# The queries of batch 2 turned by DMA instead of on TensorE, in issues between those of its keys

## The chip, the cores and the metric

The kernel runs on one core of a Trainium2 chip. Times are microseconds of the device for one execution. The engines are TensorE (PE in the profile, with its weight loads as PEld), VectorE (DVE), ScalarE (ACT), GpSimd (POOL) and SyncE (SP). GpSimd and SyncE also issue the transfers: GpSimd those that cast while they load, SyncE the stores and the transfers that transpose.

## The reference

```python
def _attn_ref(q, k, v):                      # q, k, v: (8, 8, 576, 64)
    scores = scale * np.matmul(q, k.transpose(0, 1, 3, 2))
    mask = (rel >= 0) & (rel < 64)           # rel = query position - key position
    scores = np.where(mask, scores, -1000000000.0)
    scores = scores - np.max(scores, axis=-1, keepdims=True)
    attn = np.exp(scores)
    attn = attn / (np.sum(attn, axis=-1, keepdims=True) + 1e-09)
    return np.matmul(attn, v)

def _moe_ref(x, w_in, w_out):                # (4608, 512), (512, 2048), (2048, 512)
    h = x @ w_in
    g = h * np.cos(h)
    return g @ w_out
```

A causal attention with a window of 64 over 8 batches of 8 heads and 576 positions, then two products over all 4608 rows with `h * cos(h)` between them. The input of the second part is the attention's output with the heads side by side. Inputs and output are float32.

## The kernel before

The 4608 rows are worked in nine tiles of 512 (`mt`, `MT`). For each, the first product (`first`, line 500) makes 16 blocks of 128 columns of h, ScalarE makes the sine (730), VectorE multiplies (733, the gate), and the second product (744) makes the output rows, which VectorE or ScalarE copy out and SyncE stores (509). TensorE does this without a pause while the attention of a later batch is worked between the products.

The attention of a batch goes so. GpSimd loads q, k and v in chunks of 128 positions (`load_chunk`, 183; `load_v`, 189), chunk 4 having 64. q and k are turned, so that a head's 64 numbers lie on the partitions. The scores come in two bursts (`burst_scores`, 331), the first for the query blocks 0 to 3 of 64 positions, the second for 4 to 8; a query block meets its own key block and the one before. VectorE adds the mask and takes the maximum (368), ScalarE the exponential and its sum (380), VectorE the reciprocal (390), GpSimd normalizes (397), SyncE transposes the weights by DMA (416), and TensorE multiplies them with v (`values`, 432).

q and k are turned in two ways. `turn` (244) is a DMA transpose that SyncE issues; three make one tensor of a batch, for the chunks 0 and 1, 2 and 3, and 4 (`TURNS`). k of batches 2 to 7 (`turn_k`) and q of batches 3 to 7 (`turn_q`, those in `TURNED`) go that way. q of batch 2 is transposed on TensorE: for each of four pairs of heads `tr_q` makes five transposes (227) into PSUM, and `put_q` copies them into place with two copies of VectorE (127). The turned q of a batch lies in one of two tiles, `qsets[b % 2]`; batch 2 takes that of batch 0 (`qT_75` in the order of instructions; that of the odd batches is `qT_76`).

The order of the opening (batches 0 and 1, and the first tile) is written out by hand in `FIRST`. After it, steps are entered with a due time (`at`), in which a tile has `T` = 32 units, 16 for each of its products, and `pump` writes those that are due into the program as the products go by. Each engine then takes its instructions in that order. The steps that were due before the main loop starts, the three turns of k of batch 2 among them, are written at its start, at tile 1.

SyncE and GpSimd hold their transfers in program order: one that waits for its data holds up those behind it. A transfer also waits for the landing of the one eight issues before it on the same engine.

Of the kernel before, what the change touches and what calls it, by code (L numbers as in the profile page):

```python
# [30 lines left out]
PAIRS = 4  # L31
Q = 16
T = 2 * Q
# [5 lines left out]
BUSY = 8  # L39
NB = 5  # L40
TURNS = ((0, 2), (2, 4), (4, 5))
TURNED = (3, 4, 5, 6, 7)
FAST = (7, 8)
PRODUCTS = ("P1", "P2", "P6", "P5", "P7", "P3", "P4")

# [26 lines left out]
def kernel(  # L72
# [9 lines left out]
    nc = tc.nc  # L82
    B, H, S, D = q.shape
# [17 lines left out]
    qsets = [const.tile([128, NB * PAIRS * 128], BF16, name=f"qT{i}") for i in range(2)]  # L101
# [5 lines left out]
    ident = const.tile([128, 128], BF16, name="ident")  # L107
# [6 lines left out]
    st = {}  # L114
# [11 lines left out]
    def copy(engine, out, in_):  # L126
        {"a": nc.scalar.copy, "p": nc.gpsimd.tensor_copy}.get(engine, nc.vector.tensor_copy)(out, in_)  # L127
# [29 lines left out]
    def head_rows(name, b, p):  # L157
        if (name, b) not in st:
            st[name, b] = rows_tile(name)
        lo = 2 * NC * D * p if b else RC * D + 2 * NC * D * (p - 1)  # L160
        return st[name, b][0:NP, lo:lo + 2 * NC * D].rearrange("p (h x) -> p h x", h=2)
# [48 lines left out]
    def transposed(name, b, p):  # L210
        t_ps = ps_t.tile([128, S], BF16, tag="t", name=f"t{name}_ps")
        of = st[name, b]
        if b == p == 0:
            for c in range(RC):
                for h in range(2):
                    d = slice(64 * h, 64 * h + 64)
                    nc.tensor.transpose(t_ps[d, 64 * c:64 * c + 64], of[d, 64 * c:64 * c + 64], ident[d, d])
        elif b < 2:
            rows = head_rows(name, b, p)
            for c in range(NC):  # L220
                for h in range(2):
                    nc.tensor.transpose(t_ps[64 * h:64 * h + 64, NP * c:NP * c + NP], rows[:, h, D * c:D * c + D],  # L222
                                        ident[:NP, :NP])
        else:
            for c in range(NB):
                n = min(128, S - 128 * c)
                nc.tensor.transpose(t_ps[:, 128 * c:128 * c + n], of[0:n, c, 128 * p:128 * p + 128], ident[0:n, 0:n])  # L227
        return t_ps


    def in_order(t_ps, to, b, p):
        c = RC if b == p == 0 else NC
        return t_ps.rearrange("d (c p) -> d p c", c=c), to.rearrange("d (p c) -> d p c", c=c)

    def by_pair(x):
        return x[:, 0:PAIRS * S].rearrange("d (h s) -> d h s", h=PAIRS)

    def by_chunk(x):
        return x.rearrange("d (c h p) -> d c h p", c=NB, h=PAIRS)
# [12 lines left out]
    def tr_q(b, p):  # L252
        st["tq", b, p] = transposed("q", b, p)

    def put_q(b, p, engine=None):
        if b > 1:
            t_ps, to = st.pop(("tq", b, p)), by_chunk(qsets[b % 2])[:, :, p]
            copy(engine, to[:, 0:4], t_ps[:, 0:512].rearrange("d (c p) -> d c p", c=4))
            copy(engine, to[:, 4, 0:64], t_ps[:, 512:S])
            return  # L260
        of, to = in_order(st.pop(("tq", b, p)), by_pair(qsets[b])[:, p], b, p)
        if b:
            copy(engine, to, of)
        elif engine == "a":
            nc.scalar.mul(to, of, scale)
        else:
            nc.vector.tensor_scalar(to, of, scale, None, ALU.mult)
# [4 lines left out]
    def tr_k(b, p):  # L272
        st["tk", b, p] = transposed("k", b, p)
# [327 lines left out]
    def at(time, fn, *args):  # L601
        plan.append((time, len(plan), fn, args))
# [25 lines left out]

    for b in range(2, B):
        t0 = T * (b - 1)  # L630
        for lo, hi in TURNS if b in TURNED else ():
            at(t0 - T + (24.3 if b == 4 else 23.4) + 0.01 * lo, turn_q, b, lo, hi)
        for p in range(0 if b in TURNED else PAIRS):
            t_q = t0 + (2 if b == 2 else 1) + (3.3 if b == 2 else 3.5) * p
            at(t_q, tr_q, b, p)
            at(t_q + 0.02, put_q, b, p)
        if b > 2:
            for c in range(NB):
                for i, name in enumerate(("q", "k")):
                    time = 17.9 + 2.8 * i if b == 3 and c == NB - 1 else 5.6 + 1.6 * c + 0.8 * i  # L640
                    if b > 3 and name == "k" and c > 2:
                        time = (24.2 if b == 4 else 22.4) + 0.01 * c
                    if b > 4 and c == 0:
                        time = (24.26 if b == 5 else 22.46) + 0.01 * i - T
                    at(t0 - T + time, load_chunk, name, b, c)
        for lo, hi in TURNS:
            at(t0 + 0.1 * lo - (2 if b == 2 else 6), turn_k, b, lo, hi)
        for c in range(5):
            at(t0 + (8 if b == B - 1 else 0.5) + c, load_v, b, c)
        for half_ in range(2):  # L650
            if b == 2:
                at(t0 + 24.1 + 0.01 * half_, spread_v, b, half_, "p", 0, 2)
                at(t0 + 24.2 + 0.1 * half_, spread_v, b, half_, "p", 2, 4)
            else:
                at(t0 + (24 if b == 3 else 22.2) + 0.1 * half_, spread_v, b, half_)
# [27 lines left out]
    def spread_first(lo, hi):  # L683
# [9 lines left out]
             "io": put_steps, "mk": put_masks, "mc": cast_masks,  # L693
             "tq": lambda p: tr_q(0, p), "tk": lambda p: tr_k(0, p), "Tq": lambda p: tr_q(1, p), "Tk": lambda p: tr_k(1, p),
             "pq": lambda p, engine: put_q(0, p, engine), "pk": lambda p, engine: put_k(0, p, engine),
             "Pq": lambda p, engine: put_q(1, p, engine), "Pk": lambda p, engine: put_k(1, p, engine),
             "zA": spread_first(0, 1), "zB": spread_first(1, 3), "zC": lambda engine: spread_v(0, 1, engine, 3, 4),
             "yA": lambda engine: spread_v(1, 0, engine, 0, 2), "yB": lambda engine: spread_v(1, 0, engine, 2, 3),
# [85 lines left out]
```

## Time and profile before

| | us |
|---|---|
| three runs | 301.02, 301.63, 302.92 |
| median | 301.63 |
| the profiled execution | 301.49 |
| its span, first to last instruction | 299.7 |
| mean granted clock of TensorE | 0.998 |

Where tile 1 and tile 2 lie in the span, from the timeline of TensorE:

| stretch | from, us | to, us |
|---|---|---|
| first product of tile 1, with the transposes of q of batch 2 | 57.23 | 72.98 |
| second product of tile 1, with both bursts of scores of batch 2 | 72.98 | 88.77 |
| values for tile 2 | 88.77 | 90.00 |
| first product of tile 2 | 90.00 | 103.90 |
| second product of tile 2, with the bursts of batch 3 | 103.90 | 119.24 |

In the profile's timelines a row has the start, the length, the engine (with a q for its sequencer or the queue of transfers that it issues), the line, the operation, the tiles as out<-in, and a count; what stands in brackets is idle time before it and what ended it. For a transfer the length is that of the issue; how long it takes to land stands in a line of its own. In a view of one line of the kernel the three numbers of a row are the least, the median and the largest duration in ns, and those behind them the first and the last start.

### The profile page before, as it was taken

The numbers are of one execution on the slowest core, as the hardware profiler recorded it, in microseconds if no ns is written. First come the engines' busy times: TensorE is split into PE (matmuls) and PEld (weight loads), VectorE is DVE, ScalarE is ACT, GpSimd is POOL, SyncE is SP. The second block draws the span as 40 slices with busy tenths as digits, with TensorE's granted clock in tenths as the row PEclk, the third lists the DMA queues.
The fourth block names the chain that finished last, engine by engine and source line by source line (L and its number), as shares of the span: only waits on it lengthen the run. The fifth ranks groups of instructions, "written<-read, shape, count | busy, mean of one in ns | idle before, by whom it ended". The sixth has DMA issues, their size and how long they took to land.

```text
span 299.7 us, 8184 instructions
## 1 busy us (share of the span) xinstructions
PE 291.8 (97%) x2787; PEld 159.7 (53%) x2787; DVE 230.9 (77%) x904; ACT 232.3 (77%) x781; POOL 205.2 (68%) x226
## 2 busy tenths in 40 slices
PE   8978999999999999999999999999999999999995
PEld 3667854544454444444454545444544454784584
DVE  4998788988887786788677866887588658976793
ACT  5997699876988799869986998699969996305600
POOL 9898668993699849995999599949997850000000
PEclk9999999999999999999999999999999999999999
DMA  7999999999999995999999999999999443003013
GB/s 147 175 204 191 196 190 141 113 138 148 234 165 121 202 175 99 167 143 229 152 171 139 178 164 199 142 230 165 152 121 189 70 88 142 0 3 140 3 35 107
DMA packets 165867, 43.22 MB, mean 144 GB/s; under 512 B 153216, under 2 KB 161472, under 8 KB 165824
## 3 DMA queue, kind: packets, MB, share of 16 engines
q0 software_dynamic: 100896, 18.06, 81.6%
q1 hardware_dynamic: 64784, 24.56, 45.7%
q8 instruction: 22, 0.36, 0.5%
q14 instruction: 21, 0.17, 0.2%
q10 hardware_dynamic: 144, 0.07, 0.1%
HBM read 36.70 MB, written 9.44 MB: 154 GB/s over the span
## 4 chain that ended last, share of the span: by engine, by line
PE 89%; DMA 6%; POOL 2%; DVE 0%; issue 0%; POOLq 0%
PE h_ps L500 37%; PE out_ps L744 28%; PE out_ps L587 8%; PE out_ps L483 5%; DMA w_in<-in_moe_w_in_dram 4%; PE h_ps L464 4%; PE o_ps L432 3%; PE s_ps L331 3%; DMA q<-in_q_dram 2%; POOL v L189 1%; PE s_ps L353 1%; PE tq_ps L227 0%; POOL w_in L205 0%; PE tw_ps L413 0%; POOL q L166 0%
## 5 line engine op out<-in xcount | busy, mean ns | idle before, releaser
L500 PE MATMUL h_ps<-xT,w_in 128*128 128x512 bf16 x512 | 112.5, 379 | 0.2
L733 DVE TENSOR_TENSOR gT<-h_ps,sin 128x512 bf16<-128x512 f32 x128 | 84.9, 688 | 27.3 <-ACT sin L730 27.3
L730 ACT ACTIVATE sin<-h_ps 128x512 f32<-128x512 f32 x128 | 73.8, 598 | 34.8 <-PE h_ps L500 32.6
L380 ACT ACTIVATE e<-s,negm 128x128 f32<-128x128 f32 (+1 forms) x256 | 97.2, 382 | 1.7 <-POOL v L127 0.9
L397 POOL TENSOR_TENSOR w<-e,rden 128x512 bf16<-128x512 f32 (+1 forms) x68 | 69.0, 1029 | 28.8 <-DVE rden L390 21.1
L744 PE MATMUL out_ps<-w_out,gT 128*128 128x512 bf16 x384 | 85.3, 379 | 0.0
L500 PEld LDWEIGHTS <-w_in 128*128 128x128 bf16 x512 | 49.7, 98 | 58.3
L744 PEld LDWEIGHTS <-gT 128*128 128x128 bf16 x384 | 36.5, 98 | 43.1
L368 DVE CUSTOM_DVE_ANT_0 s<-s_ps,mask 128x128 f32<-128x128 f32 (+1 forms) x256 | 56.0, 276 | 1.8 <-PE s_ps L353 1.5
L380 ACT ACTIVATION_READ_ACCUMULATOR e<-s,negm 128x1 f32 x256 | 48.3, 189 | 0.0
L189 POOL DMA_DIRECT2D v<-in_v_dram x40 | 34.1, 877 | 0.6 <-DMA q<-in_q_dram 0.6
L183 POOL DMA_DIRECT2D q<-in_q_dram x30 | 26.4, 883 | 4.6 <-PE tq_ps L222 2.6
L183 POOL DMA_DIRECT2D k<-in_k_dram x30 | 26.3, 886 | 0.6 <-DMA v<-in_v_dram 0.6
L390 DVE RECIPROCAL rden<-den 128x4 f32<-128x4 f32 (+1 forms) x73 | 12.2, 167 | 18.4 <-ACT e L380 18.1
L127 POOL COPY v<-v 64x1536 bf16<-64x1536 bf16 (+3 forms) x16 | 22.9, 1431 | 0.4
L368 DVE DVE_READ_ACCUMULATOR2_ANT negm<- 128x1 f32 x256 | 21.0, 82 | 0.1
L127 DVE CAST xT<-o_ps 128x512 bf16<-128x512 f32 x24 | 15.5, 677 | 4.7 <-PE o_ps L432 4.5
L464 PE MATMUL h_ps<-xT,w_in 128*128 128x256 bf16 x128 | 14.6, 273 | 0.9 <-DMA w_in<-in_moe_w_in_dram 0.9
L483 PE MATMUL out_ps<-w_out,gT 128*128 128x512 bf16 x64 | 14.8, 380 | 0.0
L464 PEld LDWEIGHTS <-w_in 128*128 128x128 bf16 x128 | 12.3, 98 | 2.3 <-DMA w_in<-in_moe_w_in_dram 1.0
L587 PEld LDWEIGHTS <-sums 128*128 128x128 bf16 x136 | 12.2, 98 | 2.0 <-DVE sums L532 0.4
L470 ACT ACTIVATE sin<-h_ps 128x512 f32<-128x512 f32 x16 | 9.2, 596 | 4.3 <-PE h_ps L464 4.3
(92 smaller groups left out, 293.0 us busy)
## 6 DMA issues: line engine op xcount, KB each, us to landing
out_dram<-out_sb SPq DMA_DIRECT2D x16, 512.0 KB, 8.0
v<-in_v_dram POOLq DMA_DIRECT2D x32, 128.0 KB, 6.2
q<-in_q_dram POOLq DMA_DIRECT2D x24, 128.0 KB, 9.5
k<-in_k_dram POOLq DMA_DIRECT2D x24, 128.0 KB, 9.4
w_in<-in_moe_w_in_dram POOLq DMA_DIRECT2D x4, 512.0 KB, 8.7
w_out<-in_moe_w_out_dram POOLq DMA_DIRECT2D x4, 512.0 KB, 10.9
q<-in_q_dram POOLq DMA_DIRECT2D x7, 144.0 KB, 6.2
k<-in_k_dram POOLq DMA_DIRECT2D x7, 144.0 KB, 6.3
```

Of the source, the lines that this page charges most:

```text
L127: {"a": nc.scalar.copy, "p": nc.gpsimd.tensor_copy}.get(engine, nc.vector.tensor_copy)(out, in_)
L183: nc.gpsimd.dma_start(out=st[name, b][0:n, c].rearrange("p (h d) -> p h d", h=H), in_=src.rearrange("h p d -> p h d"))
L189: nc.gpsimd.dma_start(out=vt.rearrange("p (h d) -> p h d", h=H), in_=v[b, :, c * 128:c * 128 + n, :].rearrange("h p d -> p h d"))
L368: nc.vector.tensor_tensor_reduce(out=s[:, u, c], in0=s_ps[:, u, c], in1=mask[:, 2 - j % 2 if j else 0, c], scale=-scale if b else -1.0, sc ...
L380: nc.scalar.activation(e[:, u, c], s[:, u, c], AF.Exp, bias=negm[:, u:u + 1], scale=1.0 if n < n_first else -1.0, accum_out=den[:, u:u + 1])
L397: (nc.gpsimd if engine == "p" else nc.vector).tensor_tensor(out=w[:, 0:u], in0=e[:, 0:u], op=ALU.mult, in1=rden[:, 0:u].unsqueeze(2).to_br ...
L464: nc.tensor.matmul(out=h_ps[:, half * e:half * e + half], lhsT=w_in_sb[:, ks, ff * 128:ff * 128 + 128], rhs=st["xT", 0][:, ks, half * g:ha ...
L500: nc.tensor.matmul(out=st["h", ff], lhsT=w_in_sb[:, ks, ff * 128:ff * 128 + 128], rhs=st["xT", mt][:, ks], start=start, stop=stop)
L587: nc.tensor.matmul(out=to[n_] if split else to[:, e], lhsT=lhs[name][f // 2][:, f % 2, 128 * e:128 * e + 128], rhs=rhs[name][:, f, lo:hi], ...
L730: nc.scalar.activation(sin, h_ps, AF.Sin, bias=math.pi / 2.0)
L733: nc.vector.tensor_tensor(out=gt[:, e], in0=h_ps, in1=sin, op=ALU.mult)
L744: nc.tensor.matmul(out=o_ps[e], lhsT=gT[ff // 2][:, ff % 2, ms * 128:ms * 128 + 128], rhs=w_out_sb[:, ff], start=ff == 0, stop=ff == n_ff - 1)
```

## The change

q of batch 2 is turned by DMA like those of the later batches. The list of batches to turn goes away, and with it the transposes of chunks in `transposed` and the copies in `put_q` that only batch 2 used. Each of the three turns of q of batch 2 gets a due time 0.01 before that of the turn of k of the same chunks, so that they alternate; the due times of the other batches are as before.

```diff
-TURNED = (3, 4, 5, 6, 7)
...
-        elif b < 2:
+        else:
             rows = head_rows(name, b, p)
...
-        else:
-            for c in range(NB):
-                n = min(128, S - 128 * c)
-                nc.tensor.transpose(t_ps[:, 128 * c:128 * c + n], of[0:n, c, 128 * p:128 * p + 128], ident[0:n, 0:n])
         return t_ps
...
     def put_q(b, p, engine=None):
-        if b > 1:
-            t_ps, to = st.pop(("tq", b, p)), by_chunk(qsets[b % 2])[:, :, p]
-            copy(engine, to[:, 0:4], t_ps[:, 0:512].rearrange("d (c p) -> d c p", c=4))
-            copy(engine, to[:, 4, 0:64], t_ps[:, 512:S])
-            return
...
     for b in range(2, B):
         t0 = T * (b - 1)
-        for lo, hi in TURNS if b in TURNED else ():
-            at(t0 - T + (24.3 if b == 4 else 23.4) + 0.01 * lo, turn_q, b, lo, hi)
-        for p in range(0 if b in TURNED else PAIRS):
-            t_q = t0 + (2 if b == 2 else 1) + (3.3 if b == 2 else 3.5) * p
-            at(t_q, tr_q, b, p)
-            at(t_q + 0.02, put_q, b, p)
+        for lo, hi in TURNS:
+            at(t0 - (2.01 - 0.1 * lo if b == 2 else T - (24.3 if b == 4 else 23.4) - 0.01 * lo), turn_q, b, lo, hi)
```

The queue of SyncE, from the last weights of the opening (`wT`) to the weights of the first burst of batch 2, before:

```order
L416 DMA_TRANSPOSE wT<-w 128x4x128
L244 DMA_TRANSPOSE kT<-k 128x8x128 x2
L244 DMA_TRANSPOSE kT<-k 128x4x64
L416 DMA_TRANSPOSE wT<-w 128x4x128 x2
L509 DMA out_dram<-out_sb 128x2x512 x2
L416 DMA_TRANSPOSE wT<-w 128x4x128 x4
```

and now, in the changed program, whose lines are ten fewer up to here:

```order
L406 DMA_TRANSPOSE wT<-w 128x4x128
L239 DMA_TRANSPOSE qT_75<-q 128x8x128
L239 DMA_TRANSPOSE kT<-k 128x8x128
L239 DMA_TRANSPOSE qT_75<-q 128x8x128
L239 DMA_TRANSPOSE kT<-k 128x8x128
L239 DMA_TRANSPOSE qT_75<-q 128x4x64
L239 DMA_TRANSPOSE kT<-k 128x4x64
L406 DMA_TRANSPOSE wT<-w 128x4x128 x2
L499 DMA out_dram<-out_sb 128x2x512 x2
L406 DMA_TRANSPOSE wT<-w 128x4x128 x4
```

The three turns of q have come in, one ahead of each turn of k; all that follows stands three transfers later.

VectorE in the first product of tile 1, from the last normalizing of batch 1 to the first scores of batch 2, before:

```order
L397 TENSOR_TENSOR w<-e,rden 128x512
L733 TENSOR_TENSOR gT<-h_ps,sin 128x512 x4
L127 COPY qT_75<-tq_ps 128x4x128
L127 COPY qT_75<-tq_ps 128x64
L733 TENSOR_TENSOR gT<-h_ps,sin 128x512 x3
L127 COPY qT_75<-tq_ps 128x4x128
L127 COPY qT_75<-tq_ps 128x64
L733 TENSOR_TENSOR gT<-h_ps,sin 128x512 x3
```

and now:

```order
L126 COPY out_sb<-out_ps 128x512
L387 TENSOR_TENSOR w<-e,rden 128x512
L380 RECIPROCAL rden<-den 128x4
L387 TENSOR_TENSOR w<-e,rden 128x512
L719 TENSOR_TENSOR gT<-h_ps,sin 128x512 x16
L358 ISA s,negm<-s_ps,mask 128x64
```

The eight copies of q have gone, and the sixteen gate products follow one another. On TensorE the four groups of five transposes have gone from between the products of the same stretch.

## The prediction

> **What bounds the kernel now.** I read the page's busy shares and the chain of work that ended last, then the timeline of TensorE around the place of the change.
>
> ```profile
> PE 291.8 (97%) x2787; PEld 159.7 (53%) x2787; DVE 230.9 (77%) x904; ACT 232.3 (77%) x781; POOL 205.2 (68%) x226
> PE 89%; DMA 6%; POOL 2%; DVE 0%; issue 0%; POOLq 0%
> ```
>
> TensorE is busy 291.8 of 299.7 us, and 89% of the chain is its own work. What leaves its queue in the steady part shortens the kernel by the time it took there, if nothing makes TensorE wait instead. The timeline of TensorE (start, length, line, count) shows what leaves:
>
> ```profile
> 57.23 2.75 PE L500 MATMUL h_ps<-xT,w_in 128*128 128x512 bf16 x12
> 59.82 0.52 PE L227 MATMUL tq_ps<-ident,q 128*128 128x128 bf16 x5
> 60.27 3.63 PE L500 MATMUL h_ps<-xT,w_in 128*128 128x512 bf16 x16
> 63.73 0.52 PE L227 MATMUL tq_ps<-ident,q 128*128 128x128 bf16 x5
> 64.18 2.76 PE L500 MATMUL h_ps<-xT,w_in 128*128 128x512 bf16 x12
> ...
> 72.98 0.59 PE L331 MATMUL s_ps<-kT,qT 64*64 64x64 bf16 x32
> 73.51 6.22 PE L744 MATMUL out_ps<-w_out,gT 128*128 128x512 bf16 x28
> 79.65 0.86 PE L331 MATMUL s_ps<-kT,qT 64*64 64x128 bf16 x40
> ...
> 88.77 1.20 PE L432 MATMUL o_ps<-wT,v 128*64 128x64 bf16 x64
> ```
>
> There is no idle time in brackets on any of these rows. The consumers of what is turned are the two bursts of scores of batch 2, at 72.98 and 79.65, and its values at 88.77.
>
> **The change, part by part.** *The transposes leave TensorE.* From the start of a group of five to the start of the next product it is 60.27 - 59.82 = 0.45 and 64.18 - 63.73 = 0.45 us (0.52 reaches to the modelled end of the last, which overlaps). Four such groups, two of them shown, give 1.80 us, all on the path: **-1.8 us**. That is the whole gain on offer, 0.6% of the time.
>
> *What comes next on TensorE, closed up.* Five banks of h rotate in this product, so its sixth column block needs the first gate product. I look at the rows of ScalarE and VectorE there.
>
> ```profile
> 58.79 1.28 ACT L730 ACT_TABLE_LOAD   x1
> 60.09 2.71 ACT L730 ACTIVATE sin<-h_ps 128x512 f32<-128x512 f32 x5
> 63.07 0.60 ACT L730 ACTIVATE sin<-h_ps 128x512 f32<-128x512 f32 x1 [0.27 <-PE h_ps L500]
> 60.72 2.48 DVE L733 TENSOR_TENSOR gT<-h_ps,sin 128x512 bf16<-128x512 f32 x4 [1.00 <-ACT sin L730]
> L127 DVE COPY qT<-tq_ps 128x512 bf16<-128x512 bf16 x4 | 1.6, 411 | 0.0
> ```
>
> The first sine waits for a table load until 60.09, whatever TensorE does. The first gate product ends at about 61.4 (one of the four takes 2.48 / 4 = 0.62 after 60.72). TensorE reaches the sixth block five blocks after 57.23: a block is four products, 3.63 / 16 x 4 = 0.9, less overlap (12 in 59.82 - 57.23 = 2.59, so 0.86 each), hence at 57.23 + 4.32 = 61.55. It fits by 0.1 us; I book 0. From 63.07 ScalarE waits 0.27 us for TensorE before a sine, so it follows a faster TensorE. VectorE loses four copies of 0.41 us and four small ones; it waits for sines here, so this is worth nothing by itself.
>
> *Three turns come onto SP's queue.* Its rows before, in the order of issue (start, length, count):
>
> ```profile
> 43.70 8.34 SPq L416 DMA_TRANSPOSE wT<-w  x6
> 61.36 6.30 SPq L244 DMA_TRANSPOSE kT<-k  x3
> ...
> 70.34 1.21 SPq L509 DMA_DIRECT2D out_dram<-out_sb  x2
> 78.05 5.88 SPq L416 DMA_TRANSPOSE wT<-w  x4
> ```
>
> SP is free from 52.04 to 61.36. q's first turn (chunks 0 and 1) stands ahead of k's first and can go at 52; k's first still waits until 61.3 for k's chunk 1, which is loaded here:
>
> ```profile
> L183 POOL DMA_DIRECT2D k<-in_k_dram x1: 903/903/903, 55.2 to 55.2; - x1
> DMA to landing us min/median/max: 6.1/6.1/6.1
> ```
>
> 55.2 + 6.1 = 61.3. q's first turn thus costs the later ones nothing on SP, but moves its data at about 53 to 57 beside k's loads. How full the DMA engines are there and later (a row's last two numbers are the share of their time that packets took, with overlaps, and GB/s):
>
> ```profile
> 54.00:58.00 4.00, 4.00 (x87) 2.62 (x86) 3.55 (x15) 2.58 (x9) 4.00 (x6) 1.00 1.53 97
> 70.00:74.00 4.00, 4.00 (x52) 1.92 (x50) 3.28 (x7) 2.69 (x5) 1.36 (x2) 1.00 2.53 142
> ```
>
> Bounds for what the turn delays the landing of chunk 1: 0 (it is done first) to 2.4 us (it has the engines to itself for as long as a two-chunk turn takes, below). At 1.53 they are less crowded than the 2.53 of later: I take 0.5, near the lower end.
>
> The other two q turns stand between the k turns. The three k turns, each one's row with its time to landing:
>
> ```profile
> L244 SPq DMA_TRANSPOSE kT<-k x1: 1247/1247/1247, 61.4 to 61.4; - x1
> DMA to landing us min/median/max: 6.8/6.8/6.8
> ...
> L244 SPq DMA_TRANSPOSE kT<-k x1: 2759/2759/2759, 62.7 to 62.7; - x1
> DMA to landing us min/median/max: 10.2/10.2/10.2
> ...
> L244 SPq DMA_TRANSPOSE kT<-k x1: 2099/2099/2099, 65.6 to 65.6; - x1
> DMA to landing us min/median/max: 8.5/8.5/8.5
> ...
> L416 SPq DMA_TRANSPOSE wT<-w x2: 1216/1222/1227, 67.8 to 69.1; - x2
> DMA to landing us min/median/max: 7.3/7.4/7.4
> ```
>
> They land at 68.2, 72.9 and 74.1, the weights behind them at 75.2 and 76.4. So turns overlap, one queue in order: a two-chunk turn takes 4.7 us of it beside the loads, the short one 1.2, and a turn of weights, half a two-chunk one, 1.2, so 2.4 for a two-chunk turn in a quieter stretch. The six turns of batch 3 are a second measure:
>
> ```profile
> L244 SPq DMA_TRANSPOSE qT<-q x3: 1195/1231/1243, 84.1 to 86.9; - x3
> L244 SPq DMA_TRANSPOSE kT<-k x3: 1243/1267/2392, 88.2 to 92.1; - x3
> DMA to landing us min/median/max: 3.3/4.5/5.3
> ```
>
> From the first issue at 84.1 to at most 92.1 + 5.3 = 97.4 it is 13.3 us for six, 2.2 each. Added ahead of the last k turn are one two-chunk turn (2.2 to 4.7 us; I take 3.0, between them and nearer the low end, since POOL's loads, which made the crowd, stop before 72, as its row further down shows) and one short turn (1.1 to 1.2). With the 0.5 above, the last k turn lands at 74.1 + 0.5 + 3.0 + 1.1 = 78.7; bounds 74.1 + 2.2 + 1.1 = 77.4 and 74.1 + 2.4 + 4.7 + 1.2 = 82.4.
>
> *When it is needed.* Both bursts come 1.8 us sooner. The first, at 71.2, needs chunks 0 and 1 of both: k's land at 68.2 + 0.5, so 2.5 us of cover are left. (It started at 72.98 while k's last turn was still to land at 74.1, so it waits only for the chunks that it reads.) The second starts at 79.65 - 1.8 = 77.85, and reads chunk 4 last, in its last 8 of 40 products, so at about 77.85 + 0.7 = 78.5. Against 78.7 that is a stall of 0.2 us; bounds 0 and 3.9. **+0.2 us.**
>
> *What is queued behind.* The two weight turns and the two stores go 2 to 3 us later. The weights are read at 88.77 and landed by 76.4. The first of the stores frees the buffer that takes the third pair of rows of the running tile:
>
> ```profile
> L509 SPq DMA_DIRECT2D out_dram<-out_sb x2: 509/556/602, 70.3 to 71.0; - x2
> DMA to landing us min/median/max: 7.8/8.7/9.5
> ```
>
> They landed at 70.3 + 7.8 = 78.1 and 71.0 + 9.5 = 80.5, and would at about 81 and 83.5. The copy into that buffer follows 48 products, 28 of them before the second burst and 20 after it (6.22 / 28 = 0.22 each), so it comes at 79.65 + 0.86 + 4.4 - 1.8 = 83.1, after the first store. Then come the four weight turns of the first burst, at 78.05 to 82.7:
>
> ```profile
> L416 SPq DMA_TRANSPOSE wT<-w x1: 1189/1189/1189, 82.7 to 82.7; - x1
> DMA to landing us min/median/max: 3.7/3.7/3.7
> ```
>
> The last lands at 86.4 and is read at 88.77: cover 2.3 us. Issue and use both move up by 1.8, but the queue ahead of it is later. If it lands at the old time, 0.6 us of cover are left; it stalls the values only if it lands later than 87.0. Bounds 0 and 2 us (all the added 3 to 4 us of the queue, less the cover at the old time, and less what is idle in it); I take 0.1. **+0.1 us.** POOL's loads wait for earlier landings too, but it idles afterwards:
>
> ```profile
> 76.99 1.03 POOL L397 TENSOR_TENSOR w<-e,rden 128x512 bf16<-128x512 f32 x1 [5.05 <-issue]
> ```
>
> From 71.9 to 77.0 it does nothing, which leaves over 3 us of cover with the first burst 1.8 earlier.
>
> [...]
>
> *Sum.* -1.8 + 0 + 0.2 + 0.1 = -1.5 us. The profiled execution took 301.49 us (span 299.7), 0.14 below the median of the runs, 301.63. 301.49 - 1.5 = 299.99; on the median's footing **300.1 us**.
>
> **The rivals.**
> - *The last k turn is late.* Each microsecond after 78.5 at which it lands is a microsecond of TensorE idle at the second burst; from 80.3 on the kernel is slower than before. For it: the 4.7 us that a two-chunk turn took beside the loads. At the upper bound, 82.4, the time is 301.6 - 1.8 + 3.9 = 303.7; in the middle, at 80.5, it is 301.8. Against it: the six turns in 13.3 us. This is the case on the other side.
> - *No saving reaches the end.* Something else in the opening paces TensorE, so that it idles where it transposed, or the values at 88.77 wait for weights that land no earlier: 301.6. For it: the first sine at 60.09 and only 0.1 us of room at the sixth block. Against it: ScalarE waits for TensorE from 63.07 on.
> - *Everything is hidden.* No stall at all, 301.6 - 1.8 = 299.8, which lies inside the forecast's own range.
> - *Turns don't overlap.* If each added turn took its whole time to landing, at least 6.8 us beside these loads, two would put k's last turn at 74.1 + 13.6 = 87.7, a stall of 9.2, 309.0 in all. The four landings above, 4.7, 1.2, 1.1 and 1.2 us apart though each took 7 to 10, speak against it. [...]
>
> **How the numbers follow.** A difference of 1%, 3.0 us, is about what a measurement of this kernel can tell from no change. The forecast with its hidden twin (299.4 to 300.9): 62 in 100. No saving: 13. Late k turn: 23, of which about a third beyond 302.6. Turns that don't overlap: 2. Predicted is the likeliest, 300.1. The range goes from 299.2 (the full 1.8 us and half a microsecond for the spread of the runs, 301.0 to 302.9) to 302.6, which leaves some 10 in 100 above and 5 below. Faster by over 1% (under 298.6) needs more than the 1.8 us on offer: 0.02. Slower by over 1% (over 304.6) needs a stall of 4.8 us, which takes stalls at both places or turns that don't overlap: 4 + 2 in 100, 0.06. Within 1%: 0.92.
>
> **What would show it.** TensorE's timeline goes from the gate products to the first burst without L227's rows, the burst starts near 71.2 and the second near 77.9. SP issues q's first turn near 52, k's first at 61.4 to 62, and k's last lands near 78.7. Right is the second burst with idle time under 0.5 us in front of or within it, and values near 87. Wrong is a wait for a turn of k or q over 1 us there, a wait for weights at the values, or an idle TensorE between 60 and 72. The forecast falls altogether if k's chunk 1 lands more than 3 us later than 61.3, since then the first burst waits as well.

## The result and the profile after

| | before | changed |
|---|---|---|
| runs | 20 | 20 |
| median, us | 301.31 | 303.08 |
| least to greatest, us | 300.27 to 303.99 | 300.31 to 304.74 |
| ratio, 95% interval | | 1.0055 [1.0029, 1.0081] |
| profiled execution, span, us | 301.49, 299.7 | 303.76, 302.0 |

The kernel became slower by half a percent. A second set of 12 runs beside 30 of the kernel before gave 1.0066 [1.0042, 1.0089]. Forecast was a gain of half a percent.

From the page of the changed kernel: busy shares, the granted clock in 40 slices, the chain by engine; and from its view of waits, the row of TensorE that was not there before (sum, times, longest):

```profile
PE 290.0 (96%) x2736; PEld 160.2 (53%) x2767; DVE 229.7 (76%) x896; ACT 232.5 (77%) x781; POOL 205.2 (68%) x226
PEclk9977999999999999999999999999999999999999
PE 85%; POOL 6%; DMA 3%; ACT 3%; issue 2%; DVE 1%; POOLq 0%
PE o_ps L422 <- DMA wT<-w: 1.9, 2, 1.7
```

TensorE's busy time can't be compared with that of before: twenty products were taken out, but this trace has 51 fewer, as some of its records are missing (the other profiles of the changed kernel have 2767). Its share of the chain fell from 89 to 85%, and an `o_ps` product waited. Its timeline shows where (the lines of the changed program are ten and more fewer: 490 is the first product, 321 a burst of scores, 730 the second product, 422 the values):

```profile
59.41 13.98 PE L490 MATMUL h_ps<-xT,w_in 128*128 128x512 bf16 x63
73.32 0.59 PE L321 MATMUL s_ps<-kT,qT 64*64 64x64 bf16 x32
73.84 6.22 PE L730 MATMUL out_ps<-w_out,gT 128*128 128x512 bf16 x27
79.99 0.86 PE L321 MATMUL s_ps<-kT,qT 64*64 64x128 bf16 x40
81.01 5.13 PE L730 MATMUL out_ps<-w_out,gT 128*128 128x512 bf16 x23 [0.16 <-issue]
...
89.11 0.32 PE L422 MATMUL o_ps<-wT,v 128*64 128x64 bf16 x8
89.61 0.19 PE L422 MATMUL o_ps<-wT,v 128*64 128x64 bf16 x1 [0.18 <-DMA wT<-w]
91.54 1.05 PE L422 MATMUL o_ps<-wT,v 128*64 128x64 bf16 x55 [1.74 <-DMA wT<-w]
92.61 13.97 PE L490 MATMUL h_ps<-xT,w_in 128*128 128x512 bf16 x62
```

Stretch by stretch, from the starts of these rows and of those shown of before:

| stretch | before, us | changed, us | difference |
|---|---|---|---|
| to the first product of tile 1 | 57.23 | 59.41 | +2.18 |
| first product of tile 1 | 15.75 | 13.91 | -1.84 |
| first burst to the values of tile 2 | 15.79 | 15.79 | 0 |
| values of tile 2, to the first product of tile 2 | 1.23 | 3.50 | +2.27 |
| from there to the end of the span | 209.70 | 209.39 | -0.31 |
| sum | 299.70 | 302.0 | +2.3 |

The 1.8 us came in full. Neither burst waits. The values wait for weights and give 2.27 us back. The remaining 2.18 lie in the opening, which the change touches only in its last 5 us, with the first turn of q. There the slices of the clock read 7 between 15 and 30 us (0.50 in each microsecond from 20 to 26), and executions differ anyway, as the experiments show.

The queue of SyncE in the changed kernel (start, length, count), then the landings of k's last turn, of the two stores and of the last weights:

```profile
54.34 1.23 SPq L239 DMA_TRANSPOSE qT<-q  x1
63.20 1.24 SPq L239 DMA_TRANSPOSE kT<-k  x1
64.60 1.99 SPq L239 DMA_TRANSPOSE qT<-q  x1
66.70 2.91 SPq L239 DMA_TRANSPOSE kT<-k  x1
69.70 1.39 SPq L239 DMA_TRANSPOSE qT<-q  x1
71.19 1.28 SPq L239 DMA_TRANSPOSE kT<-k  x1
72.56 2.65 SPq L406 DMA_TRANSPOSE wT<-w  x2
75.25 1.20 SPq L499 DMA_DIRECT2D out_dram<-out_sb  x2
78.38 7.41 SPq L406 DMA_TRANSPOSE wT<-w  x4
...
L239 SPq DMA_TRANSPOSE kT<-k x1: 1277/1277/1277, 71.2 to 71.2; - x1
DMA to landing us min/median/max: 7.6/7.6/7.6
...
L499 SPq DMA_DIRECT2D out_dram<-out_sb x2: 505/552/598, 75.3 to 75.9; - x2
DMA to landing us min/median/max: 8.7/9.2/9.6
...
L406 SPq DMA_TRANSPOSE wT<-w x1: 2285/2285/2285, 83.5 to 83.5; - x1
DMA to landing us min/median/max: 8.0/8.0/8.0
```

Counted from the start of tile 1's first product, so that the opening drops out: the later store lands at 75.9 + 9.6 - 59.4 = 26.1 (before 80.5 - 57.2 = 23.3), the last weights at 83.5 + 8.0 - 59.4 = 32.1 (before 86.4 - 57.2 = 29.2). The values begin at 29.7 (before 31.5). A cover of 2.3 us (time between the landing and its use) turned into a lack of 2.4: 1.8 because the use came sooner, 2.9 because the landing came later. SyncE's queue held the last weights back little: they were issued 1.4 us sooner than before (83.5 - 59.4 = 24.1 against 82.7 - 57.2 = 25.5), where their use came 1.8 sooner. But they took 8.0 us to land, not 3.7.

It is not only SyncE's transfers that are late. One load of k of batch 3, issued by GpSimd, first before, then in the changed kernel:

```profile
L183 POOL DMA_DIRECT2D k<-in_k_dram x1: 727/727/727, 80.9 to 80.9; - x1
DMA to landing us min/median/max: 5.0/5.0/5.0
```

```profile
L182 POOL DMA_DIRECT2D k<-in_k_dram x1: 727/727/727, 81.3 to 81.3; - x1
DMA to landing us min/median/max: 10.2/10.2/10.2
```

From the start of tile 1's first product it was issued 1.8 us sooner (21.9 against 23.7), took 5.2 us longer, and landed 3.4 us later (32.1 against 28.7). Transfers of both queues take longer at the same time, which speaks for a backlog in the DMA engines that is still there when the weights come; that is inferred from the landings.

### The profile page after: what moved, and what is told of

Read it like the earlier page. It is cut to its first block, busy times and chain, and to the rows that moved or that the text cites. A ratio compares the mean times of both kernels' runs of the same rounds, so it can differ in the third digit from the quotient of the medians.

```text
span 302.0 us, 8115 instructions
## 1 busy us (share of the span) xinstructions
PE 290.0 (96%) x2736; PEld 160.2 (53%) x2767; DVE 229.7 (76%) x896; ACT 232.5 (77%) x781; POOL 205.2 (68%) x226
## 4 chain that ended last, share of the span: by engine, by line
PE 85%; POOL 6%; DMA 3%; ACT 3%; issue 2%; DVE 1%; POOLq 0%
PE h_ps L490 37%; PE out_ps L730 23%; PE out_ps L577 8%; PE h_ps L454 5%; PE out_ps L473 5%; DMA wT<-w 3%; PE o_ps L422 3%; PE s_ps L321 2%; ACT e L370 2%; POOL w L387 1%; POOL v L188 1%; POOL q L165 1%; POOL k L165 1%; PE tw_ps L403 1%; PE s_ps L343 1%
## 5 line engine op out<-in xcount | busy, mean ns | idle before, releaser
L490 PE MATMUL h_ps<-xT,w_in 128*128 128x512 bf16 x497 | 111.0, 379 | 1.0
L716 ACT ACTIVATE sin<-h_ps 128x512 f32<-128x512 f32 x128 | 73.7, 599 | 33.2 <-PE h_ps L490 32.6
L387 POOL TENSOR_TENSOR w<-e,rden 128x512 bf16<-128x512 f32 (+1 forms) x68 | 68.9, 1028 | 32.4 <-DVE rden L380 24.7
L730 PE MATMUL out_ps<-w_out,gT 128*128 128x512 bf16 x372 | 83.6, 379 | 1.3 <-issue 0.9
L490 PEld LDWEIGHTS <-w_in 128*128 128x128 bf16 x512 | 50.1, 98 | 59.1
L454 PE MATMUL h_ps<-xT,w_in 128*128 128x256 bf16 x128 | 15.9, 287 | 0.0
L126 ACT CAST xT<-o_ps 128x512 bf16<-128x512 f32 x12 | 7.0, 585 | 9.9 <-PE o_ps L422 8.3
L473 PE MATMUL out_ps<-w_out,gT 128*128 128x512 bf16 x60 | 14.3, 380 | 0.3 <-issue 0.2
L454 PEld LDWEIGHTS <-w_in 128*128 128x128 bf16 x128 | 13.0, 103 | 2.0
```

The lines of the kernel that those rows point to most:

```text
L387: (nc.gpsimd if engine == "p" else nc.vector).tensor_tensor(out=w[:, 0:u], in0=e[:, 0:u], op=ALU.mult, in1=rden[:, 0:u].unsqueeze(2).to_br ...
L454: nc.tensor.matmul(out=h_ps[:, half * e:half * e + half], lhsT=w_in_sb[:, ks, ff * 128:ff * 128 + 128], rhs=st["xT", 0][:, ks, half * g:ha ...
L490: nc.tensor.matmul(out=st["h", ff], lhsT=w_in_sb[:, ks, ff * 128:ff * 128 + 128], rhs=st["xT", mt][:, ks], start=start, stop=stop)
L716: nc.scalar.activation(sin, h_ps, AF.Sin, bias=math.pi / 2.0)
L730: nc.tensor.matmul(out=o_ps[e], lhsT=gT[ff // 2][:, ff % 2, ms * 128:ms * 128 + 128], rhs=w_out_sb[:, ff], start=ff == 0, stop=ff == n_ff - 1)
```

## Experiments

The theory: the added turns leave the DMA engines a backlog, behind which the weights of the first burst land after TensorE wants them. The first rival: the opening itself is slower in the changed program. Others are named with the runs. All ratios are to the kernel before, run on the same chip in the same session. "Wait" is the length of the values of tile 2 less the 1.23 us that they take, and landings are counted from the start of tile 1's first product; both are of the one profiled execution, the medians of all. The wait of the run with columns set to zero holds some 0.6 us of slow products, as its paragraph shows.

| run | median, us | ratio, 95% interval | last weights land | values begin | wait |
|---|---|---|---|---|---|
| changed kernel again | 303.78 | 1.0066 [1.0042, 1.0089] | 32.0 | 29.7 | 2.2 |
| no turns of q at all | 299.48 | 0.9931 [0.9907, 0.9956] | 28.4 | 29.7 | 0 |
| turns added to before | 302.12 | 1.0008 [0.9981, 1.0035] | 32.7 | 31.5 | 1.0 |
| a store moved behind | 300.68 | 0.9963 [0.9936, 0.9990] | 31.1 | 29.7 | 1.3 |
| q's turns first | 301.19 | 1.0003 [0.9981, 1.0024] | 31.4 | 29.7 | 1.6 |
| columns set to zero | 304.06 | 1.0093 [1.0059, 1.0126] | 32.8 | 29.7 | 3.5 |
| q first, store behind | 300.03 | 0.9959 [0.9931, 0.9988] | 30.9 | 29.7 | 1.1 |
| half by DMA | 301.81 | 1.0015 [0.9995, 1.0035] | 29.5 | 31.1 | 0 |
| wait filled | 302.47 | 1.0050 [1.0021, 1.0079] | 32.7 | 31.4 | 1.1 |
| fourth weights on TensorE | 300.85 | 0.9975 [0.9950, 0.9999] | 32.4 | 29.9 | 2.4 |
| all three moves | 299.29 | 0.9917 [0.9886, 0.9948] | 29.4 | 29.9 | 0 |

**The changed kernel again.** No edit.

> The changed kernel once more. Theory (the weights' turns of the first burst are late, so the values of tile 2 wait): from the start of tile 1's first product the first burst comes after 13.9 us, and TensorE idles 1 to 3 us at the values of tile 2 before their products run; time 302 to 304 us. The 2.2 us by which tile 1 began later in the profiled execution (59.4 instead of 57.2) are the opening's own scatter, with the granted clock below 1 between 20 and 40 us: another execution begins tile 1 between 57 and 59. Rival (the opening itself is slower in the changed program): tile 1 begins at 59.4 again, at a full clock too.

Tile 1's first product began at 57.72 and the mean clock was 0.999, so the opening's 2.18 us are not the program's. The first burst came after 13.91 us, and the values took 3.41 us. This execution took 301.99 us, near the least of its 12: a wait of 2.2 against a gain of 1.84 explains +0.4, not the +2 of the median. That difference is taken up further down.

**The gain alone.**

```diff
-        for lo, hi in TURNS:
+        for lo, hi in TURNS if b > 2 else ():
             at(t0 - (2.01 - 0.1 * lo if b == 2 else ...), turn_q, b, lo, hi)
...
     nc.vector.memset(small, 0.0)
+    nc.vector.memset(qsets[0][:, PAIRS * S:], 0.0)
```

> The changed kernel without any turning of q of batch 2: its three turns are left out, so that the scores of batch 2 are taken with what batch 0 left in that tile, and the output is not the reference's; 256 columns that nothing wrote before are set to zero once. Theory (the turns' load on the queue is what costs): no wait at the values of tile 2, weights land with 2 us of cover as before, time 299.5 us, ratio to before 0.994. Rival (the opening is slower, or the closed-up product is paced by something else): 301 to 303 us without the turns too.

299.48 us, as expected. The last weights land 1.3 us ahead of the values, which run without a break:

```profile
86.49 1.20 PE L422 MATMUL o_ps<-wT,v 128*64 128x64 bf16 x64
87.72 8.58 PE L490 MATMUL h_ps<-xT,w_in 128*128 128x512 bf16 x39
```

So the closed-up product gives its 1.8 us to the end of the kernel, and what costs is the turning.

**The cost alone.** The kernel before, plus the three turns into a tile that nothing reads.

```diff
+    spare = const.tile([128, 3, PAIRS, 128], BF16, name="spare")
...
+    def turn_spare(b, lo, hi):
+        n, c = min(128, S - 128 * lo), lo // 4 * 2
+        to = spare[:, c:c + hi - lo, :, 0:n].rearrange("d c h p -> d (c h) p")
+        nc.sync.dma_start(out=to, in_=st["q", b][0:n, lo:hi].rearrange("p c x -> p (c x)"), transpose=True)
...
+        for lo, hi in TURNS if b == 2 else ():
+            at(t0 - 2.01 + 0.1 * lo, turn_spare, b, lo, hi)
```

> The kernel before, with its transposes on TensorE, and in addition the three turns of q of batch 2, alternating with those of k, into a spare tile that nothing reads. Theory (late weights): TensorE up to the second burst as before; the last weights of the first burst, which landed 2.3 us ahead of the values, land 2.8 us later against them than before, so that the values wait 0.5 us, between 0 and 2; time 301.8 us, ratio 1.002. Rival (the turns as such are harmless, the opening costs): no wait, 301.3 us. If the turns delayed the bursts too, 303 or more.

TensorE's rows up to the second burst keep their distances of before. The values wait:

```profile
88.09 0.34 PE L438 MATMUL o_ps<-wT,v 128*64 128x64 bf16 x9
89.29 1.05 PE L438 MATMUL o_ps<-wT,v 128*64 128x64 bf16 x55 [0.85 <-DMA wT<-w]
90.36 5.99 PE L506 MATMUL h_ps<-xT,w_in 128*128 128x512 bf16 x27
```

The last weights land at 32.7 instead of 29.2. The turns alone, with nothing gained, use up the 2.3 us of cover and 1.0 us more in this execution; the median rises by 0.6 us, within what the interval allows for nothing.

**A store moved behind the weights.**

```diff
-        at(T + 8.1 + 0.1 * m, store, st.pop(("osb", m)), 0, 2 * m, 0, 2)
+        at(T + (22.9 if m else 8.1), store, st.pop(("osb", m)), 0, 2 * m, 0, 2)
```

> The changed kernel, with the second of the two stores of tile 0 (512 KB) moved behind the four weight turns of the first burst on SyncE's queue. Theory (the weights stand behind the stores in one queue): the weights land about 2 us sooner, the wait at the values falls from 1.9 to under 0.5 us, time 300.5 us. Rival (the loads of GpSimd crowd the DMA engines, and the place of a store changes little): the wait stays over 1.2 us, time 302.5 to 303.

```profile
88.16 0.34 PE L422 MATMUL o_ps<-wT,v 128*64 128x64 bf16 x9
89.63 1.05 PE L422 MATMUL o_ps<-wT,v 128*64 128x64 bf16 x55 [1.13 <-DMA wT<-w]
90.70 5.56 PE L490 MATMUL h_ps<-xT,w_in 128*128 128x512 bf16 x25
```

The median fell by 3.1 us to 300.68, as the theory said; the wait in the profiled execution fell only to 1.3, between the two. That execution took 302.72, one of the slowest of its twelve. The last weights landed at 31.1, but in the five profiles of the changed kernel itself they landed at 31.1 to 33.2, so this one profile doesn't show what the place of the store is worth to the landing. The median does show that it counts.

**q's turns first.**

```diff
-            at(t0 - (2.01 - 0.1 * lo if b == 2 else ...), turn_q, b, lo, hi)
+            at(t0 - (2.51 - 0.1 * lo if b == 2 else ...), turn_q, b, lo, hi)
```

> The changed kernel with q's three turns due ahead of k's first, so that they stand q, q, q, k, k, k on SyncE's queue, in the gap before k's chunks land. Theory (what counts is the transfers' work left in the crowded stretch, from some 4 to 32 us after the start of tile 1's first product): most of q's turning is done by 4 us after that start, the last weights land near 30 us after it, against 32.1 in the changed kernel; the wait at the values falls from 2.2 to under 0.8 us, time 300.3 to 301.3. Rival (any further transfer delays the weights by its whole length, wherever it stands): the wait stays at 2 us. Second rival (q's turns take the engines from k's loads): k's first turn starts over 1.5 us later and the first burst waits.

The time is as expected (301.19), the landing less so: 31.4, not 30. q's second and third turn landed at 8.4 and 9.7 instead of 14.0 and 18.2, and k's last at 17.7 instead of 19.4, yet the last load of GpSimd landed at 34.2 instead of 32.0. The work seems to have only changed places in the crowd; with landings of 31.1 to 33.2 in the changed kernel's own profiles, one profile can't tell.

**The same setting to zero, alone.**

```diff
     nc.vector.memset(small, 0.0)
+    nc.vector.memset(qsets[0][:, PAIRS * S:], 0.0)
```

> The changed kernel with nothing but the setting to zero of 256 columns that the run without any turn had in its opening. For the part of the loss that the wait at the values doesn't hold (the changed kernel's granted clock was below 0.998 in most executions, in the run without turns in none). Theory (whether TensorE's clock is held back for a few us in the opening hangs on the opening's phase, not on the turns): the clock is 1.0 in most executions, the wait at the values is 2.2 us as before, time 302.2. Rival (the change brings it about): clock below 0.998 in most, time 303.5.

The theory on the opening's phase falls: the clock was below 0.997 in 5 of 6 executions, against none of 7 in the run without turns, which has the same edit. So it is not the opening's phase that keeps the clock up there. Here the half clock comes at the values; the last of them:

```profile
90.08 1.66 PE L422 MATMUL o_ps<-wT,v 128*64 128x64 bf16 x55 [1.23 <-DMA wT<-w]
```

These 55 took 1.66 us, against 1.05 to 1.09 in the profiles of the changed kernel. The mean clock was 0.70 between 88 and 92 (0.50 in the second half of it) and 0.87 between 92 and 96, which is half the clock for 2.4 and 1.0 us: it began near 89.6, before the wait was over. Of the 3.5 us in the table some 0.6 are thus slow products, and the wait was 2.9.

**Both moves.** The diffs of the store and of q's turns together.

> q's three turns ahead of k's, and the second store of tile 0 behind the weights of the first burst: both moves together. Theory: no wait at the values (under 0.2 us), time 299.8 to 300.2. Rival (a move is worth nothing beside the other, since a third thing holds the weights): a wait of over 1 us, time over 301.

300.03 us, inside the expected span, though 1.1 us of wait were left in the profiled execution. The kernel is now faster than before by 0.4%.

**Half by DMA.** The kernel before; q's chunks 0 and 1 by DMA, the others on TensorE.

```diff
-            for c in range(NB):
+            for c in range(2, NB):
...
-            copy(engine, to[:, 0:4], t_ps[:, 0:512].rearrange("d (c p) -> d c p", c=4))
+            copy(engine, to[:, 2:4], t_ps[:, 256:512].rearrange("d (c p) -> d c p", c=2))
...
+        if b == 2:
+            at(t0 - 2.01, turn_q, b, 0, 2)
```

> The kernel before, in which only the chunks 0 and 1 of q of batch 2 are turned by DMA, ahead of k's first turn, in the gap of SyncE's queue; the chunks 2, 3 and 4 stay on TensorE. Theory: the first product of tile 1 takes 15.0 us instead of 15.75 (four times two transposes of 0.09), the turn is over before the crowded stretch, no wait at the values, time 300.8. Rival (also this turn delays all behind it): a wait of 0.5 us or more at the values, 301.5.

```profile
90.11 1.20 PE L432 MATMUL o_ps<-wT,v 128*64 128x64 bf16 x64
91.34 6.85 PE L500 MATMUL h_ps<-xT,w_in 128*128 128x512 bf16 x31
```

No wait, and weights with 1.6 us of cover: in this execution the first turn, which runs before the crowd, cost the weights almost nothing (29.5 against 29.2). The first product took 15.31 us, a gain of 0.44 and not of 0.75: three transposes still take 0.34. By the starts of the single transposes, here and in the trace of before, the dear one is that of chunk 4, with its 64 rows. It starts 0.15 us after the one before it, and the next product 0.13 after it, while transposes of 128 rows follow each other every 0.056. Yet the median, 301.81 instead of the expected 300.8, shows no gain; in the profiled execution the opening ran to 59.02. That part is scatter or unexplained.

**The wait filled.**

```diff
-    def keep_busy(n):
-        ps_busy = bank("O0", "busy")
+    def keep_busy(n, which="O0"):
+        ps_busy = bank(which, "busy")
...
+    at(T * 2 - 1.011, keep_busy, 8, "O1")
     for mt in range(2, n_mt):
```

> The changed kernel with eight products of 0.22 us, whose result nothing reads, on TensorE right ahead of the values of tile 2, where it waited for weights: 1.7 us of filling inside a wait of 2.2. Theory (a wait of 2 to 3 us at the values also brings TensorE's clock to half for 3.4 us afterwards in part of the executions, which costs 1.7 us more; a mean clock of 0.994 is one such stretch, 0.989 two): with the wait filled the clock is 0.997 or more in about as many executions as in the kernel before (43 of 59), and the time falls by about 1 us to 302.3, though TensorE has more to do. Rival (the clock is lost in the opening, as in the first profile of the changed kernel): below 0.997 in most as before, time 303.3 or more.

```profile
88.27 1.89 PE L133 MATMUL busy<-w_out 128*128 128x512 bf16 x8
90.08 0.34 PE L422 MATMUL o_ps<-wT,v 128*64 128x64 bf16 x9
91.37 1.05 PE L422 MATMUL o_ps<-wT,v 128*64 128x64 bf16 x55 [0.94 <-DMA wT<-w]
```

With 1.7 us more on TensorE the kernel took 302.47, against the changed kernel's 303.1 to 303.8. But its ratio, 1.0050, lies within both intervals of the changed kernel, so a gain in time is not shown. The clock was 0.997 or more in 7 of 12 executions (one of these took 1694 us and is not in the ratio). In the changed kernel it was so in 4 of 32, in the kernel before in 62 of 83. So the clock held more often, as the theory said.

**Where the clock is lost.** Three more executions of the changed kernel.

> The changed kernel, one more profiled execution, to see where TensorE's clock is halved. Theory (the wait at the values brings it about): a stretch of 3.4 us at half the clock begins within 4 us of the start of the values of tile 2, and the first products of tile 2 run in 0.43 us. Rival (the opening loses it): the half clock lies before 30 us, none at the values.

> The same once more, for the same question; of three such executions the theory expects one or two with a half clock behind the wait, the rival none.

> The same a third time; the wait itself is 1.5 to 3.5 us in each of the three.

The first two, 303.11 and 301.05 us, had a full clock, a wait of 1.3 and 2.5 us, and tile 1's first product began at 59.7 and 56.4. The third, 305.29 us, lost clock in both places. Its clock by slices, its timeline at the values, and busy times between 92 and 96 (the third number from the end is the granted clock):

```profile
PEclk9979999999997999999999999999999999999999
...
88.56 0.22 PE L422 MATMUL o_ps<-wT,v 128*64 128x64 bf16 x3 [0.36 <-DMA wT<-w]
89.73 0.19 PE L422 MATMUL o_ps<-wT,v 128*64 128x64 bf16 x1 [0.95 <-DMA wT<-w]
91.50 1.09 PE L422 MATMUL o_ps<-wT,v 128*64 128x64 bf16 x55 [1.58 <-DMA wT<-w]
92.57 5.61 PE L490 MATMUL h_ps<-xT,w_in 128*128 128x512 bf16 x18
...
92.00:96.00 4.00, 4.00 (x45) 1.74 (x38) 1.78 (x4) 1.87 (x2) 2.72 (x3) 0.57 1.03 147
```

A clock of 0.57 over 4 us is half the clock for 3.4 of them, if the low clock was 0.50 as in the first profile and in that of the kernel that set columns to zero, right behind a wait of 3.4 us: 18 products took 5.61 us, where 0.22 each is 3.9. The kernel that set columns to zero shows the same at the end of its wait of 2.9 us. The waits of 1.3 to 2.5 us in four other profiles of the changed kernel were not followed by one. Neither was a wait of 2.8 us in the opening of the first of these three, at the values of tile 1, which is also why its tile 1 began late:

```profile
57.90 0.66 PE L422 MATMUL o_ps<-wT,v 128*64 128x64 bf16 x30 [2.81 <-DMA wT<-w]
```

Whether the first turn of q, issued right behind these weights, has a part in that no run shows. In the two waits that were followed by a half clock nine products ran ahead of and between the pauses, none of which was over 1.6 us, while the unbroken 2.8 us were not followed by one; what decides it no run shows.

**The fourth weights on TensorE.**

```diff
-    direct = set(range(n_first)) | {n_first + i for i in DIRECT} | set(last)
+    fourth = n_listed + 3
+    direct = set(range(n_first)) | {n_first + i for i in DIRECT} | set(last) | {fourth}
...
-            st["tw", n] = t_ps = ps_t.tile([128, GF, 128], BF16, tag="t", name="tw_ps")
+            pool, tag = (ps, "S") if n == fourth else (ps_t, "t")
+            st["tw", n] = t_ps = pool.tile([128, GF, 128], BF16, tag=tag, name="tw_ps")
...
+            elif n == fourth:
+                at(T * b - 4.2, g_trans, n)
+                at(T * b - 4.15, g_put, n)
             else:
                 at(time + lags[4], g_trans, n)
```

> The changed kernel, in which the fourth group of weights of the first burst of batch 2, the last to land, is transposed on TensorE instead of by DMA (0.31 us of TensorE, one copy of VectorE). Theory (the values wait for the last of the four to land): they wait for the third instead, some 1.3 to 1.9 us sooner; wait 0.4 to 1.2 us, time 302. Rival (something else than the weights holds the values): wait 2 us, 303.5.

300.85 us, better than expected, but its profiled execution was its slowest (303.0 us): the third weights landed at 32.4 there and the wait was 2.4. So the median moved the way the theory said, and further, while a shorter wait is not shown.

**All three moves.** The diffs of q's turns, the store and the fourth weights.

> All three moves: q's turns ahead of k's, the second store of tile 0 behind the weights, and the fourth group of weights on TensorE. Theory: the third weights land 29.5 us after the start of tile 1's first product, and are read at 30.0: no wait, clock as in the kernel before, time 299.3, ratio 0.993. Rival (each move is eaten by a later wait): over 300.5.

```profile
87.01 1.20 PE L424 MATMUL o_ps<-wT,v 128*64 128x64 bf16 x64
88.23 7.07 PE L492 MATMUL h_ps<-xT,w_in 128*128 128x512 bf16 x32
```

299.29 us, ratio 0.9917 [0.9886, 0.9948], no wait. This beats both kernels and equals the run without turns, 299.48: with the weights out of the backlog the change keeps its gain. The moves were not tried on the kernel before; there the values didn't wait, so nothing was to be saved at this place.

## Why the prediction was wrong, step by step

- *"-1.8 us" on TensorE*: right, 1.84. The run without turns shows that it reaches the end.
- *"It fits by 0.1 us; I book 0"* at the sixth block: right; the first product runs unbroken.
- *VectorE's copies, nothing*: nothing in the runs speaks against it.
- *"Bounds for what the turn delays the landing of chunk 1 ... I take 0.5"*: nothing in this execution. k's first turn was issued 3.8 us after tile 1's start, before 4.1.
- *"That is a stall of 0.2 us" at the second burst*: none, in all five profiles of the changed kernel. k's last turn landed 19.4 us after tile 1's start, where the step had 78.7 - 57.2 = 21.5. It landed 2.5 us later than before (16.9), where the step booked 4.6.
- *"Bounds 0 and 2 us ...; I take 0.1" for the weights*: this step failed. It was 2.3 us in the first profiled execution, 1.3 to 3.4 over five, mean 2.3. The step counted the earlier use, which left 0.6 us of cover, but it let the weights land at the old time and looked for a delay only in the queue ahead of them. The issue was not what was late: the last weights were issued 24.0 to 25.4 us after tile 1's start in the five profiles, before 25.5, but took 7.0 to 8.0 us to land, before 3.7. That the turns would lengthen the landing of transfers behind them was the missing part: in the run without turns the last weights took 4.8 us to land, and nothing waited. The step's bounds, 0 and 2, lay too low as well. This cover of 2.3 us was the smallest of the transfers that the prediction lists, and 1.8 and 2.9 together exceeded it.
- *What no step had*: the clock. It was halved for 3.4 us behind the wait in one of five profiled executions of the changed kernel, and in the one of the kernel that set columns to zero. With the wait filled a full clock was more frequent, 7 of 12 against 4 of 32.
- *The rivals*: "no saving reaches the end" named this very wait, with 13 in 100, but ended at the price of the old time, since it let the weights land no earlier rather than later. "The last k turn is late" had 23 in 100; no profile shows it.

What stays open is how the median's +1.8 to +2.2 us divides. The wait less the gain accounts for about 0.5. Executions at like clocks can be compared: at 0.997 or more the changed kernel's six average 302.2 us, the 62 of the kernel before 301.4; near 0.994 it is 302.9 (17) against 301.8 (15). So about 1 us is there at an equal clock, twice what the wait explains, and the rest goes with a full clock being rarer, 6 of 35 with the three further executions, against 62 of 83. Where the half clocks lie is known for the five profiles alone: two of them lost clock in the opening, one of these behind the wait too. The counts of the other runs don't follow the wait alone: a full clock came in 9 of 12 with the turns added to before, 4 of 12 with the store moved, and 6 of 12 with half by DMA, which had no wait. The start of tile 1 varied from 56.4 to 59.7 us, even at a full clock. Nor was it tried to take GpSimd's loads out of the crowd, which would have parted the engines' load from the order of SyncE's queue; the medians of the moved store and the late loads speak for a part of both.

## What to carry to other kernels

A transfer added to a crowded stretch can be paid for by the transfer with the least cover behind it, as here, where 2.3 us of cover became a lack of 2.4, and not by its own consumer. So list all landings up to the next quiet moment with the time of their use, and move the uses up by the gain before judging the cover. Work taken from the bounding engine makes every cover on its path shorter by the same amount, here 1.8 us, so the tightest one decides whether the gain is kept. The gain can be saved by clearing that one place, here by sending the tightest weights another way, a store behind them and q's turns ahead (299.29 us against 303.1 to 303.8).

## What the runs showed that was not expected

- 576 KB turned by DMA made the weights behind them land about 3 us later (32.1 against 29.2), though the last added turn was issued 13.8 us ahead of the last weights. A load of the other queue took 10.2 us instead of 5.0.
- Two waits of TensorE came with further lost time: behind one of 3.4 us and from the end of one of 2.9 us on its clock was halved for 3.4 us (means of 0.57 over 4 us, and of 0.70 and 0.87 over 4 us each). After waits of 1.3 to 2.8 us it was not, in four profiles.
- A transpose of 64 rows cost TensorE more than one of 128. Of the 0.45 us of a group of five, 0.28 lie between the start of the fourth, a full one, and the next product; full ones follow each other every 0.056 us.
